# Block-sparse attention and a bilinear feed-forward: a planner's matmul times and margins taken anew

## The chip, the cores and the metric

The kernel runs on one core of a Trainium2 chip. Each engine of the core works through its own list of instructions in order: PE multiplies matrices, DVE and ACT work element by element and move results out of PE's accumulators, POOL gathers blocks of keys, SP and ACT issue DMA transfers. Engines wait for each other and for transfers on semaphores. The metric is the device time of one launch in microseconds (us). The median of three runs of the kernel before is 862.08 us (860.63 to 865.51).

## The reference

Four batches of eight heads attend over 768 positions with 64 numbers per head. Positions fall into 24 blocks of 32, and a block of queries sees few blocks of keys; what comes out is laid side by side into 3072 tokens of 512 numbers, and a feed-forward follows.

```
B, H, S, D = q.shape                       # 4, 8, 768, 64
scores = q @ k.transpose / sqrt(D)
mask = (|blk_i - blk_j| <= 1) or blk_i in (0, 23) or blk_j in (0, 23)
for qb in range(24):
    for kb in sampled_blocks[qb]:          # three random blocks
        mask[qb, kb] = True
attn = softmax(where(mask, scores, -1e9))
x = (attn @ v).reshape(3072, 512)
out = ((x @ w_a) * (x @ w_b)) @ w_out      # w_a, w_b: 512 x 1536, w_out: 1536 x 512
```

## The kernel before

Every matrix is held as a high and a low fp16 part, and each product is three matmuls (high by high, low by high, high by low). The work falls into two sorts.

**Attention** goes by units, one for each block of 32 queries of a batch with all eight heads: 96 units. Unit n of batch b has the name b*24+i; those with i = 0 and i = 23 are dense (all 24 key blocks), the others have eight gathered blocks. For a unit POOL gathers key columns (`KG`, L629 to L634), SP loads gathered value rows (`VG`, L656 to L669), PE makes scores (L1031 the mask, L930 the products: the task S), DVE takes a minimum (`low`), ACT the exponentials (`sm`, L1056), ACT and DVE split the weights into parts (`hl`, L948 to L955), the DMA or PE turns them (`pt`, L1081 or L1109), and PE multiplies them with the values (L974: the task A). Two helpers write the attention into `xT` (L1241 on ACT, L1244 on DVE).

**The feed-forward** goes by 12 chunks of 256 tokens (eight units), three of a batch, and by 12 slices of the inner dimension. Task P of a chunk and slice makes both first products in `ab` (L1273, 24 matmuls); ACT and DVE multiply them into `a` (L1290, L1293) and split the result into `gh` and `gl` (L1302, L1305); task O multiplies these with w_out (L1333 to L1335, 6 matmuls). P of a chunk needs all of the chunk's units. "P3_0" is chunk 3, slice 0; "A31" the values of unit 31. PE fills waits in one chunk's units with tasks of earlier chunks.

At the start the weights are loaded, put into 32-bit words from two halves (L775 to L782 on DVE), scaled, and split into parts (L806 to L823), slice by slice; keys and values of the first batch the same way; and tables of the sampled blocks are made (`make_tables`, L405: loads L421 to L428 on ACT's queue, then L433 to L463 on DVE). `offs`, which the gather of keys needs, comes from the first table, the mask `mrows` from the second. Weights of later slices are loaded and converted among the first units.

The order on each engine is not written by hand. When the kernel is built, a class `Plan` (L133) simulates all flows with given times: `pe(ns, fn)` asks for the matmul engine for so many ns, `dve`, `act`, `pool`, `sp` and `load_way` for the others. It picks what can start first, with a rank as the tie-break, and writes instructions in that order. On the chip the order is fixed, and real durations and real semaphores decide. The numbers in the plan never reach the chip. The constants `LATE_*` are margins: an event is said to be later than the simulated time by that much, so what needs it is put further back. `GATE_*` and `LEAD_*` say how many units ahead loads begin. The plan also models eight lanes of DMA transfers (`LANES`) and the two levels of PE's clock (`array`, L182).

```
at = max(ready, self.free.get(way.eng, 0.0))
if way.moved:
    at = max(at, self.dma - DMA_AHEAD, self.generator)
    if len(self.landed) >= LANES:
        at = max(at, self.landed[-LANES])
```

The transfers of the chip go by eight semaphores in turn (DMAHW0 to DMAHW7), so a transfer is issued only when the one that had the same semaphore eight issues earlier has landed, and an issue that has to wait holds up what is queued behind it on its engine.

Of the kernel before, what the change touches and what calls it, by code (L numbers as in the profile page):

```python
# [53 lines left out]

LATE_PT, LATE_VG, LATE_AV, LATE_G = 2500, 2500, 1500, 700
LATE_S = 1000
LATE_HL, LATE_KS, LATE_Q = 2500, 2500, 2000
DMA_AHEAD = 1750
X_HIGH, X_UNITS = 600, 16

# [180 lines left out]
def load_way(moved, fn):  # L241

    return [Way("LOAD", 475, fn, moved)]
# [7 lines left out]
def kernel(  # L251
# [238 lines left out]
    def keys(b, g):  # L490
        yield from gate(first_of[b] - GATE_KV)
        raw, freed = yield from raw_tile(b, g, 0)
        yield load_way(1000, lambda: nc.scalar.dma_start(raw, k[b, g]))
        if g + 1 < NG:
            plan.start(keys(b, g + 1), first_of[b] - LEAD_K)
        elif b > 0:
            plan.start(values(b, 0), first_of[b] - LEAD_V)
        t = raw.rearrange("p (t d) -> p t d", d=D)
        done = yield from take("ks", KS_BUFS)
        ks = work.tile([P, 2 * NT, P], F16, tag="ks", name=f"ks{b}_{g}", bufs=KS_BUFS)  # L500
        at = at_k + b * NG + g
        s = scale[:, at : at + 1]
        yield act(1020, lambda: nc.scalar.activation(
            ks[:, :, :D], t, AF.Abs, accum_out=bound[:, at : at + 1]
        ))
        end = yield from set_scale(slice(at, at + 1), FLOOR_QK)
        k_scale[b].fire(end)
        yield act(930, lambda: nc.scalar.activation(ks[:, :, :D], t, AF.Copy, scale=s))
        end = yield dve(1070, lambda: nc.vector.scalar_tensor_tensor(
            ks[:, :, D:], t, s, ks[:, :, :D], ALU.mult, ALU.subtract  # L510
        ))
        freed.fire(end)
        if b == 0:
            ends = Event(2)
            for h in range(2):
                plan.start(turn_keys(g, h, ks, ends, done), first_of[b] - LEAD_K, end)
            return
        if b == 1:
            yield w_freed
        if b >= 2:  # L520
            yield k_free[b - 2]
        end = yield sp(1700, 2200, lambda: nc.sync.dma_start_transpose(
            keysT[b % 2][:, 2 * g : 2 * g + 2, :].rearrange("p h (t s) -> p (h t) s", s=P),
            ks.rearrange("p t d -> p (t d)"),
        ))
        done.fire(end + LATE_KS)
        k_ready[b].fire(end + LATE_KS)
# [31 lines left out]
    def values(b, g):  # L559

        yield from gate(first_of[b] - GATE_KV)
        raw, freed = yield from raw_tile(b, g, 1)
        yield load_way(1000, lambda: nc.scalar.dma_start(raw, v[b, g]))
        if g + 1 < NG:
            plan.start(values(b, g + 1), first_of[b] - LEAD_V)
        elif b + 1 < B:
            plan.start(keys(b + 1, 0), first_of[b + 1] - LEAD_K)
# [21 lines left out]
            vd[b][:, g * 4 * D : (g + 1) * 4 * D].rearrange("(t p) x -> p t x", p=P),  # L589
            vs.rearrange("p t a x -> p t (a x)"),  # L590
        ))
        done.fire(end)
        v_stored[b].fire(end)

    def values_scale(b):
        yield v_bound[b]
# [136 lines left out]
    def turn_queries(cc, a):  # L733

        end = yield sp(650, 700, lambda: nc.sync.dma_start(
            QT[cc][D:, 1 - a], QT[cc][:D, a]
        ))
        q_ready[cc].fire(end)


    def raw_weights(n, count):
# [218 lines left out]
    def values_into(b, i, quads, first, last):  # L960
# [22 lines left out]
                for g in (2 * hq, 2 * hq + 1):  # L983
                    pair_sums(g, terms)

        t = yield pe(sum(len(terms) for _, terms in quads) * 180 + 80, sums)
        if last and quads[-1][0] == HQ - 1:
            av_done[b, i].fire(t)
            if i % 2:
# [24 lines left out]
    def attend(b, i):  # L1014
# [24 lines left out]
            for hq in range(HQ):  # L1039
                scores(ps[:, hq], cc, i, hq, lambda h: kg[:, h], False)  # L1040

        t = yield pe(850, all_scores)
        kg_free[kn].fire(t)
        next_unit(b, i, t - HOP)
        mx = low[:, at, :, 0]
# [85 lines left out]
    def attend_quad(b, i, hq, ends):  # L1131
# [14 lines left out]
            )  # L1146

        for x in range(2):
            t = yield pe(450, lambda x=x: half_scores(x))
        if hq == 0:  # L1150
            quad_sent[b, i].fire(t - HOP)
        else:
# [103 lines left out]
    def first_products():  # L1256
        plan.start(second_products(), R_P2)
        for cc, f in in_order:
# [18 lines left out]
                                skip_group_check=True,  # L1277
                            )

            t = yield pe(2680, products)  # L1280
            if f == NF - 1:
                ffn_done[cc].fire(t)
            plan.start(inner(cc, f, ab, read), R_NOW, t)
# [28 lines left out]
    def second_products():  # L1312
        banks, o_read = [None] * NJ, [None] * NJ
        sums = [{} for _ in range(NC)]
        for cc, f in in_order:
# [18 lines left out]
                    mm(po, gh[:, js], wol[:, f, :], start=False, stop=False)  # L1334
                    mm(po, gl[:, js], wos[:, f, :], start=False, stop=(f == hi - 1))  # L1335

            t = yield pe(1290, products)
            if f == hi - 1:
                for j in range(NJ):
                    plan.start(  # L1340
# [123 lines left out]
```

## Time and profile before

| | before |
|---|---|
| median of 3 runs | 862.08 us (860.63 to 865.51) |
| the profiled execution's own time | 856.35 us |
| its span, first to last instruction | 854.6 us |
| mean granted clock of PE | 0.966 of full speed |
| PE busy | 763.1 us (89%) |
| DVE busy | 587.0 us (69%) |
| ACT busy | 501.3 us (59%) |

All durations that follow are from the one profiled execution; its own time is 1.75 us above its span and 0.7% under the median. The span has three stages. In the first, up to some 190 us, weights and keys are converted while the first units run; in the second PE has attention and feed-forward tasks side by side; in the third, from some 750 us, only the feed-forward's last tasks are left.

### The profile page before, as it was taken

The numbers are of one execution on the slowest core, as the hardware profiler recorded it, in microseconds if no ns is written. First come the engines' busy times: TensorE is split into PE (matmuls) and PEld (weight loads), VectorE is DVE, ScalarE is ACT, GpSimd is POOL, SyncE is SP. The second block draws the span as 40 slices with busy tenths as digits, with TensorE's granted clock in tenths as the row PEclk, the third lists the DMA queues.
The fourth block names the chain that finished last, engine by engine and source line by source line (L and its number), as shares of the span: only waits on it lengthen the run. The fifth ranks groups of instructions, "written<-read, shape, count | busy, mean of one in ns | idle before, by whom it ended". The sixth has DMA issues, their size and how long they took to land.

```text
span 854.6 us, 24181 instructions
## 1 busy us (share of the span) xinstructions
PE 763.1 (89%) x9192; PEld 568.3 (66%) x9192; DVE 587.0 (69%) x1589; ACT 501.3 (59%) x1158; POOL 179.5 (21%) x428
## 2 busy tenths in 40 slices
PE   2256478799999979999999999999999999999998
PEld 1134366577767757767777867777777677777775
DVE  4999989998687568775677786755767876332222
ACT  6688779776675467684475765843845663232222
POOL 0642332300043133120034240200422310000000
PEclk9985589999999999999999999999999999999999
DMA  8767795577957589987676989667677767500000
GB/s 270 227 192 238 237 237 183 156 145 180 203 150 173 123 189 236 187 191 174 151 184 150 177 208 226 149 180 165 158 164 152 146 147 150 129 25 2 26 1 25
DMA packets 187758, 136.89 MB, mean 160 GB/s; under 512 B 130681, under 2 KB 155258, under 8 KB 187642
## 3 DMA queue, kind: packets, MB, share of 16 engines
q1 hardware_dynamic: 175712, 97.56, 51.7%
q10 hardware_dynamic: 11930, 37.79, 14.5%
q8 instruction: 72, 1.18, 0.6%
q14 instruction: 44, 0.36, 0.1%
HBM read 86.28 MB, written 12.58 MB: 116 GB/s over the span
## 4 chain that ended last, share of the span: by engine, by line
PE 62%; DVE 16%; DMA 9%; ACT 6%; issue 3%; SPq 2%; POOL 1%; ACTq 0%; POOLq 0%; DVEq 0%
PE ab L1273 33%; PE av L974 7%; PE o L1333 6%; PE o L1335 6%; PE o L1334 5%; PE s L930 4%; DMA VG<-vd 3%; DVE hl L955 2%; ACT sm L1056 2%; DMA keysT<-ks 2%; DVE xT L1244 2%; DVE low L1046 1%; DVE QT L711 1%; ACT QT L709 1%; PE s L1031 1%
## 5 line engine op out<-in xcount | busy, mean ns | idle before, releaser
L1273 PE MATMUL ab<-xT,wab 128*128 128x256 f16 x3456 | 403.8, 274 | 2.4 <-DVE a L1293 1.8
L1273 PEld LDWEIGHTS <-wab 128*128 128x128 f16 x3456 | 336.2, 98 | 67.8 <-issue 10.2
L1293 DVE SCALAR_TENSOR_TENSOR a<-a,to_g,ab 128x256 f32<-128x256 f32 x144 | 68.7, 478 | 116.5 <-ACT a L1290 115.0
L1290 ACT ACTIVATE a<-ab,w 128x256 f32<-128x256 f32 x144 | 67.3, 468 | 128.0 <-PE ab L1273 126.5
L1056 ACT ACTIVATE sm<-s,low,cq 128x256 f32<-128x256 f32 x176 | 97.8, 558 | 49.1 <-DVE low L1049 25.4
L629 POOL COPY KG<-keysT 128x384 int32<-128x384 int32 x88 | 57.0, 647 | 308.0 <-PE s L930 279.7
L974 PEld LDWEIGHTS <-VG 128*128 128x128 f16 x2688 | 99.2, 101 | 29.5 <-issue 20.2
L974 PE MATMUL av<-pt,VG 128*128 128x64 f16 x2688 | 105.4, 197 | 15.0 <-ACT pt L1115 6.9
L1333 PE MATMUL o<-woh,gh 128*128 128x512 f16 x288 | 109.7, 381 | 2.4 <-ACT gh L1302 2.4
L1335 PE MATMUL o<-wos,gl 128*128 128x512 f16 x288 | 109.2, 379 | 2.8 <-DVE gl L1305 2.8
L1334 PE MATMUL o<-wol,gh 128*128 128x512 f16 x288 | 109.2, 379 | 0.0
L955 DVE SCALAR_TENSOR_TENSOR hl<-sm,den,hl 128x256 f16<-128x256 f32 (+1 forms) x208 | 104.6, 510 | 3.3 <-ACT hl L948 1.5
L634 POOL COPY KG<-keysT 128x128 int32 x264 | 92.0, 385 | 45.2 <-issue 23.3
L1302 ACT ACTIVATE gh<-a 128x256 f16<-128x256 f32 x144 | 59.4, 413 | 57.6 <-DVE a L1293 55.0
L1305 DVE SCALAR_TENSOR_TENSOR gl<-gh,a 128x256 f16<-128x256 f16 x144 | 63.0, 438 | 29.7 <-ACT gh L1302 28.4
L1244 DVE SCALAR_TENSOR_TENSOR xT<-av,xT 64x256 f16<-64x256 f32 x96 | 40.4, 421 | 40.9 <-ACT xT L1241 40.1
L930 PE MATMUL s<-KG,QT 128*32 128x256 f16 x1408 | 59.6, 293 | 9.3 <-POOL KG L634 7.5
L1046 DVE TENSOR_REDUCE low<-s 128x2 f32<-128x512 f32 x88 | 60.0, 683 | 8.3 <-PE s L930 7.6
L1241 ACT ACTIVATE xT<-av 64x256 f16<-64x256 f32 x96 | 36.1, 376 | 42.5 <-PE av L974 41.3
L930 PEld LDWEIGHTS <-QT 128*32 128x32 f16 x1664 | 43.8, 102 | 18.2 <-issue 7.7
L1335 PEld LDWEIGHTS <-gl 128*128 128x128 f16 x288 | 28.1, 98 | 39.7 <-DVE gl L1305 6.9
L948 ACT ACTIVATE hl<-sm,den 128x256 f16<-128x256 f32 (+1 forms) x86 | 43.9, 514 | 9.9 <-DMA pt<-hl 2.5
(116 smaller groups left out, 771.7 us busy)
## 6 DMA issues: line engine op xcount, KB each, us to landing
VG<-vd SPq DMA_DIRECT2D x284, 64.0 KB, 2.3
VG<-vd SPq DMA_DIRECT2D x88, 192.0 KB, 3.1
VG<-vd SPq DMA_DIRECT2D x32, 384.0 KB, 3.7
q<-in_q_dram ACTq DMA_DIRECT2D x24, 256.0 KB, 5.1
QT<-QT SPq DMA_DIRECT2D x24, 256.0 KB, 3.3
vd<-vs SPq DMA_DIRECT2D x16, 384.0 KB, 3.1
out_dram<-ou SPq DMA_DIRECT2D x24, 256.0 KB, 2.3
stage<-in_k_dram ACTq DMA_DIRECT2D x12, 384.0 KB, 4.4
```

The lines of the kernel that those rows point to most:

```text
L634: nc.gpsimd.tensor_copy(to[:, :, (5 + r) * w : (6 + r) * w], of[:, :, bass.ds(at, w)])
L930: mm(to[h * BLK : (h + 1) * BLK], q_block(cc, i, 4 * hq + h, a), rhs(4 * hq + h), start=(first and a == 0), stop=(a == 1), skip_group_chec ...
L955: t = yield dve(221 + n * 1.03, lambda: nc.vector.scalar_tensor_tensor(lo, sm, over, hi, ALU.mult, ALU.subtract))
L974: mm(av[:, g, i % 2, :], w, pt[:, y, cols], start=(i % 2 == 0 and g == 0 and first and n + m == 0), stop=(last and n == len(terms) - 1 and ...
L1046: yield dve(685, lambda: nc.vector.tensor_reduce(mx, ps, axis=mybir.AxisListType.X, op=ALU.max, negate=True))
L1056: t = yield act(750, lambda hq=hq: nc.scalar.activation(sm[:, hq], ps[:, hq], AF.Exp, bias=low[:, at, hq, 0:1], scale=cq[:, cc, hq : hq + ...
L1273: mm(ab[:, i, :], wab[:, f, i, part, kt, :], xc[:, kt, a, :], start=(i == 0 and kt == 0 and part + a == 0), stop=(kt == KT - 1 and a == 1) ...
L1290: yield act(470, lambda: nc.scalar.activation(a_sb, ab[:, 0, :], AF.Copy, scale=w3[:, f : f + 1]))
L1293: t = yield dve(420, lambda: nc.vector.scalar_tensor_tensor(a_sb, a_sb, to_g[:, n : n + 1], ab[:, 1, :], ALU.mult, ALU.mult))
L1333: mm(po, gh[:, js], woh[:, f, :], start=(f == lo), stop=False)
L1334: mm(po, gh[:, js], wol[:, f, :], start=False, stop=False)
L1335: mm(po, gl[:, js], wos[:, f, :], start=False, stop=(f == hi - 1))
```

## The change

Times that the plan takes for PE's tasks are set anew, and margins are added or made longer. No instruction of the chip's is written differently; what changes is when the plan believes that things are ready, and with it the order of the instructions and which engine takes a step that can go to either.

```diff
-LATE_HL, LATE_KS, LATE_Q = 2500, 2500, 2000
+LATE_HL, LATE_KS, LATE_Q = 2500, 4000, 2000
+LATE_KV, LATE_VD, LATE_QT = 1500, 2000, 1000
...
         yield load_way(1000, lambda: nc.scalar.dma_start(raw, k[b, g]))
+        yield LATE_KV
...
         yield load_way(1000, lambda: nc.scalar.dma_start(raw, v[b, g]))
+        yield LATE_KV
...
-        done.fire(end)
-        v_stored[b].fire(end)
+        done.fire(end + LATE_VD)
+        v_stored[b].fire(end + LATE_VD)
...
-        q_ready[cc].fire(end)
+        q_ready[cc].fire(end + LATE_QT)
...
-        t = yield pe(sum(len(terms) for _, terms in quads) * 180 + 80, sums)
+        t = yield pe(sum(len(terms) for _, terms in quads) * 165 + 60, sums)
...
-        t = yield pe(850, all_scores)
+        t = yield pe(690, all_scores)
...
-            t = yield pe(450, lambda x=x: half_scores(x))
+            t = yield pe(385, lambda x=x: half_scores(x))
...
-            t = yield pe(2680, products)
+            t = yield pe(2650, products)
...
-            t = yield pe(1290, products)
+            t = yield pe(1310, products)
```

Three places show what becomes of the order. Lines of the kernel after are one to three higher than before. The numbers at the end of names tell buffers apart and differ between the two.

The first place is ACT's list in the first microseconds. Before, behind the loads of values (`wab_73<-in_v_dram`):

```order
L563 DMA wab_73<-in_v_dram 128x768
L508 ACTIVATE ks0_1_123<-wab_73,scale_94 128x12x64
L563 DMA wab_73<-in_v_dram 128x768
L421 DMA mrow_118<-in_sampled_blocks_dram 1x144
L425 DMA mbox_117<-in_sampled_blocks_dram 24x6
L428 DMA mbox_117<-c_blocks 24x29
L755 DMA stage_77<-in_moe_w_a_dram 128x1024
L508 ACTIVATE ks0_2_125<-wab_73,scale_94 128x12x64
```

After, behind the copies of the transposed keys (`keysT0`), and ahead of the second slice's weights:

```order
L574 ACTIVATE va0_2_247,bound_v_92<-wab_73 128x768
L758 DMA stage_77<-in_moe_w_a_dram 128x1024
L809 ACTIVATE wab_73,bound_91<-wab_73 128x2x512
L422 DMA mrow_118<-in_sampled_blocks_dram 1x144
L426 DMA mbox_117<-in_sampled_blocks_dram 24x6
L429 DMA mbox_117<-c_blocks 24x29
L758 DMA stage_77<-in_moe_w_b_dram 128x1024
L809 ACTIVATE woh_74,bound_91<-w2_196 128x512
```

The three loads of the sampled blocks and constants (`mrow`, `mbox`) stood between conversions of keys (`ks0`), and now stand behind the Square of the first slice of weights (L809, before L806). On DVE the table work that follows them stood ahead of the first weights, and now stands behind them.

The second place is ACT's list at the units 8 to 12 of the first batch, with the semaphores that a row waits for. `stage_77` and `keysT1_79` are where weights land, `q2` the queries of chunk 2, `sm11` the exponentials of unit 11. Before:

```order
L693 DMA q2_1406<-in_q_dram 64x1024 [waits DMAHW4_49]
L693 DMA q2_1406<-in_q_dram 64x1024 [waits DMAHW7_49]
L811 ACTIVATE woh_74<-w17_1088,scale_94 128x512
L948 ACTIVATE hl9_1409<-sm9_1344,den_98 128x256 [waits DMAHW6_49,Activation_49]
L823 ACTIVATE wos_76<-woh_74 128x512 [waits Activation_49]
L948 ACTIVATE hl9_1409<-sm9_1344,den_98 128x256
L948 ACTIVATE hl10_1418<-sm10_1376,den_98 128x256 [waits DMAHW1_49,DVE_49]
L755 DMA stage_77<-in_moe_w_b_dram 128x1024 [waits DMAHW3_49]
L1056 ACTIVATE sm11_1495,den_98<-s11_1372,low_97,cq_96 128x256 [waits DVE_49,PE_49]
L1056 ACTIVATE sm11_1495,den_98<-s11_1372,low_97,cq_96 128x256
```

After:

```order
L696 DMA q2_1404<-in_q_dram 64x1024 [waits DMAHW3_49]
L696 DMA q2_1404<-in_q_dram 64x1024 [waits DMAHW4_49]
L951 ACTIVATE hl9_1409<-sm9_1335,den_98 128x256 [waits DVE_49,Activation_49]
L758 DMA stage_77<-in_moe_w_b_dram 128x1024 [waits DMAHW6_49,DMAHW0_49]
L814 ACTIVATE wab_73<-wab_73,scale_94 128x2x512 [waits DVE_49]
L758 DMA stage_77<-in_moe_w_out_dram 128x1024 [waits DMAHW7_49,DVE_49]
L951 ACTIVATE hl9_1409<-sm9_1335,den_98 128x256 [waits Activation_49]
L951 ACTIVATE hl8_11_1408<-sm8_11_1262,den_98 128x384
L814 ACTIVATE woh_74<-w17_1152,scale_94 128x512
L809 ACTIVATE woh_74,bound_91<-w20_1224 128x512
L1059 ACTIVATE sm11_1500,den_98<-s11_1371,low_97,cq_96 128x256 [waits DVE_49,PE_49]
L951 ACTIVATE hl10_1432<-sm10_1378,den_98 128x256 [waits DMAHW1_49]
```

The load of w_b stood directly ahead of `sm11` and now stands seven rows ahead of it, with conversions and the load of w_out between them, and it waits for other lanes.

The third place is ACT's list around the end of chunk 2's slices (`a2_9` to `a2_11`, `gh2_9` to `gh2_11`) and the units 35 to 38 (`sm35` ...), shortly ahead of chunk 3's first product. Before:

```order
L1302 ACTIVATE gh2_11_5294<-a2_11_5237 128x256
L1056 ACTIVATE sm35_5315,den_98<-s35_5101,low_97,cq_96 128x256 x2
L1360 ACTIVATE ou2_0_5339<-o2_0_0_4165,to_out_104 128x512
L704 ACTIVATE QT5_5242,bound_91<-q5_5178 64x2048
L1056 ACTIVATE sm36_5420,den_98<-s36_5191,low_97,cq_96 128x256 x2
L1241 ACTIVATE xT0_88<-av1_6_5290 64x4x64 x2
L1056 ACTIVATE sm37_5456,den_98<-s37_5331,low_97,cq_96 128x256
L878 ACTIVATE junk_105,bound_91<-xT0_88 128x1024
L493 DMA stage_77<-in_k_dram 128x768
L709 ACTIVATE QT5_5242<-q5_5178,scale_94 64x2048
L1056 ACTIVATE sm37_5456,den_98<-s37_5331,low_97,cq_96 128x256
```

After:

```order
L1293 ACTIVATE a2_9_5235<-ab2_9_5026,w3_99 128x256
L1059 ACTIVATE sm36_5282,den_98<-s36_5094,low_97,cq_96 128x256
L1305 ACTIVATE gh2_9_5289<-a2_9_5235 128x256
L1059 ACTIVATE sm36_5282,den_98<-s36_5094,low_97,cq_96 128x256
L1293 ACTIVATE a2_10_5280<-ab2_10_5236,w3_99 128x256
L712 ACTIVATE QT5_5107<-q5_5095,scale_94 64x2048
L1305 ACTIVATE gh2_10_5350<-a2_10_5280 128x256
L951 ACTIVATE hl34_5284<-sm34_5043,den_98 128x256
L1293 ACTIVATE a2_11_5375<-ab2_11_5290,w3_99 128x256
L494 DMA stage_77<-in_k_dram 128x768
L1244 ACTIVATE xT0_88<-av1_6_5182 64x4x64 x2
L951 ACTIVATE hl35_5293<-sm35_5208,den_98 128x256
```

Before, the last slice's `gh2_11` stood ahead of `sm35`; now `gh2_9` to `gh2_11` stand among and behind `sm36`. On PE the order before was A30, S37, A31, S38, P3_0; after it is A30, S37, P2_11, S38, A31, two O tasks of chunk 2, A32, P3_0, and then the last O task of chunk 2.

## Rows read from the trace of the kernel before

**Rows 1.** Busy us by stretch: PE, PEld, DVE, ACT, POOL, PEclk, DMA share, GB/s.

```profile
100.00:150.00 50.00, 39.44 (x516) 30.25 (x516) 45.87 (x119) 41.32 (x90) 15.35 (x31) 0.86 0.74 209
...
200.00:750.00 550.00, 537.58 (x6759) 400.63 (x6755) 384.45 (x1079) 321.51 (x780) 119.64 (x309) 1.00 0.77 170
```

**Rows 2.** Waits of PE, 200 to 750 us: line, releaser, us, times, longest.

```profile
PE av L974 <- DMA VG<-vd: 3.3, 6, 1.0
PE o L1333 <- ACT gh L1302: 2.2, 2, 1.7
PE s L930 <- DMA QT<-QT: 1.9, 3, 1.3
PE ab L1273 <- DVE a L1293: 1.8, 2, 1.2
PE s L1031 <- ACT sm L1056: 1.0, 2, 0.8
PE o L1335 <- DVE gl L1305: 0.9, 2, 0.6
PE av L974 <- DMA pt<-hl: 0.8, 2, 0.4
PE ab L1273 <- DVE xT L1244: 0.6, 1, 0.6
```

**Rows 3.** Timeline of ACT, the start: issues of table loads; first weight Square.

```profile
10.71 0.54 ACTq L421 DMA_DIRECT2D mrow<-in_sampled_blocks_dram  x1
...
28.65 1.06 ACT L806 ACTIVATE wab<-wab 128x1024 f16<-128x1024 f32 x1 [0.56 <-DVE wab L782]
```

**Rows 4.** Timeline of DVE, the start.

```profile
17.57 0.17 DVE L433 TENSOR_SCALAR mrow<-mrow 1x72 f32<-1x72 int32 x1
...
20.91 0.28 DVE L463 CAST mrows<-mbox 24x256 bf16<-24x256 f32 x1
...
34.39 0.67 DVE L1046 TENSOR_REDUCE low<-s 128x2 f32<-128x512 f32 x1
...
36.70 2.96 DVE L584 SCALAR_TENSOR_TENSOR vs<-wab,scale,vs 128x768 f16<-128x768 f32 x3
...
44.77 0.51 DVE L955 SCALAR_TENSOR_TENSOR hl<-sm,den,hl 128x256 f16<-128x256 f32 x1
```

**Rows 5.** Timeline of PE, the start.

```profile
31.21 1.04 PE L930 MATMUL s<-KG,QT 128*32 128x256 f16 x16 [4.57 <-POOL KG L634]
```

**Rows 6.** Groups of DVE by line and shape, 0 to 165 us: busy, mean ns.

```profile
L951 DVE TENSOR_SCALAR hl<-sm,den 128x256 f16<-128x256 f32 x7 | 2.4, 348 | 0.1
...
L550 DVE COPY keysT<-kt 128x768 f16<-128x768 f16 x4 | 2.2, 546 | 0.0
...
L1116 DVE COPY pt<-pt_t 128x1024 f16<-128x1024 f16 x2 | 1.4, 685 | 0.0
L951 DVE TENSOR_SCALAR hl<-sm,den 128x384 f16<-128x384 f32 x3 | 1.3, 431 | 0.0
```

**Rows 7.** Timelines at 114 us: ACT, and last DVE.

```profile
114.33 0.35 ACTq L755 DMA_DIRECT2D stage<-in_moe_w_b_dram  x1
114.79 0.56 ACT L1056 ACTIVATE sm<-s,low,cq 128x256 f32<-128x256 f32 x1 [5.39 <-DMA VG<-vd]
...
116.02 0.17 DVE L1061 TENSOR_SCALAR den<-den 128x2 f32<-128x2 f32 x1 [3.56 <-ACT sm L1056]
```

**Rows 8.** Timeline of PE, 308 to 317 us.

```profile
308.45 0.39 PE L1333 MATMUL o<-woh,gh 128*128 128x512 f16 x1 [1.70 <-ACT gh L1302]
...
312.88 0.77 PE L974 MATMUL av<-pt,VG 128*128 128x64 f16 x21 [0.95 <-DMA VG<-vd]
...
316.29 2.97 PE L1273 MATMUL ab<-xT,wab 128*128 128x256 f16 x16 [0.60 <-DVE xT L1244]
```

**Rows 9.** Busy us in ten-us stretches, columns as in rows 1.

```profile
300.00:310.00 10.00, 8.00 (x122) 5.41 (x119) 5.62 (x15) 4.45 (x13) 2.99 (x10) 1.00 1.06 191
310.00:320.00 10.00, 7.64 (x117) 5.74 (x116) 7.71 (x25) 9.13 (x19) 3.90 (x10) 0.83 0.72 195
```

## The prediction, made before the result was known

> **What bounds the kernel now.** I read the busy times by stretch first, because the stages have different limits. From 100 to 150 us DVE is busy 45.87 of 50 us and PE 39.44, at a granted clock of 0.86: here DVE's list of conversions sets the pace, and PE waits for it. From 200 to 750 us PE is busy 537.58 of 550 us, at full clock [rows 1]. In that middle stage a change of order can win only what PE waits, 12.4 us. The waits of PE there say for what: 3.3 us for gathered values, 2.2 for `gh`, 1.9 for queries turned by DMA, 1.8 for `a`, 1.0 for exponentials, 0.9 for `gl`, 0.8 for turned weights, 0.6 for `xT` [rows 2], which add up to 12.5 us. What is left after 750 us is matmuls without a partner; no number of the change reaches it. So there are three places to look at: the start, where the order on ACT and DVE counts; the long stall that ACT shows in its timeline near 114 us; and PE's waits in the middle, of which a third lie in eight microseconds, as the timeline of PE shows.
>
> **The start.** Before, the load of the sampled blocks is issued at 10.71 us [rows 3] and the tables' first conversion starts at 17.57 us, so it has taken at most 6.9 us until it could be used; the last table row starts at 20.91 and ends at 21.19 [rows 4], so the block is some 3.6 us long. After, ACT issues that load behind the first Square of the weights. This Square starts at 28.65 us before [rows 3]; without the tables ahead of its input it can start up to 3.6 us sooner, at some 25 us, and the issue follows at some 26. With 6.2 to 6.9 us until use, three short conversions (0.5 us) and a gather of 4 us (PE waited 4.57 us for the one ahead of the first scores [rows 5]), S0 starts at some 37.4 us in place of 31.21, 6.2 us later. What hides part of that is that DVE has work, and it now does it first: 2.96 us of conversions of values stand before S0's reduction that stood behind it, and two conversions of weights (1.5 us, between 34.39 and 36.70) as well. The distance from S0's reduction (34.39) to the second half of `hl0` (44.77) [rows 4] shrinks by these 4.5 us, and the lag there is 6.2 - 4.5 = 1.7. In the DVE-bound stage that is what counts. I take +1.7, with bounds of 0 (the load lands fast and DVE is never idle) and +6.2 (all of the lag stays).
>
> **Conversions that go to the other engine.** Steps that ACT or DVE can do are put down anew. Up to chunk 1's first product DVE loses one copy of keys (0.546 us), four conversions of `hl` of 0.348, two copies of `pt` of 0.685 and two conversions of dense `hl` of 0.431, in all 4.17; it gains one copy of `pt` and five of `hl`, 2.42 [rows 6]. DVE is lighter by 1.75 us, ACT heavier by some 2 to 3 us. ACT is busy 41.32 of 50 us where DVE is busy 45.87 [rows 1], so the ACT work finds room. I take -1.75; bounds -1.75 and 0.
>
> **The stall at 114 us.** ACT stands idle 5.39 us ahead of `sm11`, put down to a load of gathered values; the row before it is the issue of w_b's load at 114.33 [rows 7], which has to wait for the transfer eight issues earlier. `sm11` is queued behind the issue, DVE's L1061 needs its sums and waits 3.56 us for them [rows 7]. In a stage that DVE bounds, that is the price. After, the load of w_b stands seven rows ahead of `sm11` and waits for an earlier transfer, since the lanes fall otherwise. What can be late next is the load of w_a behind `sm11`, which waits for a query load, ahead of chunk 2's `QT`. I take 0.8 us of the 3.56 as left: -2.8; bounds -3.6 and 0.
>
> These three make -2.85 for the start of the middle stage.
>
> **The chunk boundary at 308 to 317 us.** PE waits 1.70 us for `gh`, 0.95 for the values of unit 31, 0.80 for exponentials and 0.60 for `xT` ahead of chunk 3's first product, 4.05 us in eight [rows 2, 8]. The new order puts P2_11 between S37 and A31, and A31, two O tasks and A32 ahead of P3_0: between the write of `xT` by unit 31 and P3_0 there is now PE work of two O tasks and a unit's values, where there was one S. That covers 0.60, and 0.95 is covered by P2_11. `gh2_11` no longer stands alone in front: O tasks of chunk 2 are left over as fill. I take 3.3 of the 4.05 as gone; bounds 0 and -4.05. Behind this cluster the granted clock falls: 0.83 in the stretch 310 to 320 and 1.00 ahead [rows 9]. That is 3.4 us at the lower level, 1.7 lost. It comes with a PE that was busy 8.00 and then 7.64 of ten us. If the cluster goes, I expect this to go: -1.7; bounds -1.7 and +1.7 (another such fall elsewhere).
>
> **The other waits in the middle.** Of 3.3 + 1.9 + 0.8 us for values, queries and turned weights [rows 2], 0.95 is in the cluster; 5.05 are left. The new margins (values stored and turned queries later in the plan) and shorter times of A and S let the plan issue more of the attention ahead, so that most loads of values have more PE work behind them. I take half: -2.5; bounds 0 and -5.05. Against that stands that every order has waits of its own that its plan does not see, and a fresh order has fresh ones: the old one has 12.5 us in 550. Take from it the 3.3 and 2.5 that I count as gone, and 6.7 remain; that the new order brings half as many again, +3.5, is my choice; the bounds are 0 and +12.5 (as many as before, all new).
>
> A rule of the Trainium skill bears on this. Rows first: in 300 to 310 us the DMA engines are busy 1.06 of their time by the records, while PE waits for values at 312.88 [rows 8, 9]. "DMA: Bandwidth & Descriptors", section "Issuing engines are not separate DMA queues", says that transfers started by any of the engines run on the same 16 DMA engines and interleave. By it the lateness would be a matter of bytes in that stretch and not of the order of issue, and the -0.95 and the -2.5 would not come; that case is a rival below.
>
> **The sum.** 1.7 - 1.75 - 2.8 - 3.3 - 1.7 - 2.5 + 3.5 = -6.85 us. The profiled execution took 856.35 us, which becomes 849.5; the ratio is 0.992. The profiled execution was 0.7% faster than the median of the runs shown, so I put the ratio on the median: 862.08 x 0.992 = 855.2 us. The best end: no lag at the start, -1.75, -3.6, all 12.5 of the waits, -1.7, in all -19.55, by the same ratio 842.4 us.
>
> **The rivals.**
> *No change.* The gain at 114 us and the one at the boundary come, but waits come back elsewhere, because the DMA engines are the limit around 300 to 340 us (1.06 busy, above) and because a later S0 eats the start: 1.7 - 1.75 - 2.8 - 1.5 (half of the boundary and nothing of the clock) + 4 of new waits = -0.35, so 861.7 us. For it: the DMA share in the middle is 0.77 over 550 us [rows 1], and the bytes are the same. Against it: 0.77 is no limit over the whole, only in stretches.
> *Slower.* The late tables. Its place is S0: when the load of the sampled blocks lands as late as I worked out, the whole lag of 6.2 us goes through DVE, because each unit needs S, `sm` and `hl` one after the other. Nothing else gained: 862.08 x (856.35 + 6.2)/856.35 = 868.3 us. It decides if DVE stands idle for more than 4 us between 25 and 45 us. For it: where DVE sets the pace [rows 1], each microsecond in which it has nothing to do is lost. Against it: the 4.5 us of work moved ahead.
> *A large gain.* All waits of the middle go: 842 to 845 us. Against it: no order so far is free of waits.
>
> **Chances.** The forecast 0.50, no change 0.25, the late tables 0.20, the large gain 0.05. A measurement of this kernel can tell about 0.5% (4.3 us) from no change, so faster means below 857.8 and slower above 866.4. The forecast with its own range of 849 to 859 lies in "faster" with 0.45 and in "same" with 0.05; the late tables give 0.18 to "slower" and 0.02 to "same". Faster 0.45 + 0.05 = 0.50, same 0.05 + 0.25 + 0.02 = 0.32, slower 0.18. The range goes from the middle of the large gain, 844, to the late tables' 868.
>
> **What would show it.** In the profile after: S0 starts at about 37 us, with DVE idle for about 2 us ahead of it; ACT has no idle row above 2 us between 105 and 120 us; the first product of chunk 3 starts some 6 to 9 us sooner than 316.29 [rows 8], and the stretch that holds it has a granted clock of 1.00 and PE busy above 9 of ten; PE's waits from 200 to 750 us add up to 8 to 10 us. It would be wrong if `hl0`'s second half came more than 4 us later than 44.77, if the w_b load, or the w_a load behind `sm11`, stood on ACT's queue for 3 us again, or if the waits for values in the middle grew above 6 us.

## The result, and the profile after

| | before | after |
|---|---|---|
| median, 4 runs of each in one comparison | 863.63 us (860.63 to 865.51) | 850.43 us (850.02 to 857.9) |
| ratio of the runs | 1 | 0.988 (0.9834 to 0.9926) |
| the profiled execution's own time | 856.35 us | 850.74 us |
| its span | 854.6 us | 849.0 us |
| PE busy in the span | 763.1 us (89%) | 759.4 us (89%) |

The kernel is 1.2% faster; 855.2 us had been forecast. The spans of the two profiles differ by only 5.6 us where the medians differ by 13.2, since the profiled execution of before was shorter than any of its four runs here. Both kernels were therefore profiled a second time (experiments 9 and 12). A ratio leaves out runs over 1.5% longer than the fastest of the same kernel in that comparison (none here, three of six in experiment 11, whose median of all six is 861.62 us).

The busy times by stretch of the kernel after, with the columns of [rows 1]; the first two answer to the two shown of before:

```profile
100.00:150.00 50.00, 35.07 (x454) 27.03 (x444) 42.13 (x107) 37.09 (x81) 18.55 (x33) 0.72 0.86 186
200.00:750.00 550.00, 546.33 (x6895) 409.29 (x6894) 386.47 (x1086) 331.75 (x802) 121.65 (x309) 1.00 0.77 172
100.00:130.00 30.00, 15.07 (x189) 11.18 (x179) 23.88 (x61) 17.82 (x38) 12.19 (x20) 0.56 1.04 199
300.00:350.00 50.00, 48.80 (x651) 36.34 (x649) 37.45 (x114) 33.32 (x82) 15.79 (x41) 1.00 0.93 205
350.00:750.00 400.00, 398.20 (x5080) 299.61 (x5079) 273.30 (x768) 231.50 (x568) 81.98 (x208) 1.00 0.74 166
```

From 100 to 150 us PE is busy 35.07 us in place of 39.44, and the granted clock is 0.72 in place of 0.86: the start became worse, against the forecast. From 200 to 750 us PE is busy 546.33 in place of 537.58: the middle gained 8.75. The last three rows are for comparison with the same stretches before:

```profile
100.00:130.00 30.00, 21.25 (x258) 15.95 (x259) 26.09 (x70) 22.44 (x49) 11.88 (x24) 0.77 0.88 233
300.00:350.00 50.00, 44.86 (x653) 32.87 (x650) 39.08 (x116) 34.13 (x85) 18.12 (x47) 0.97 0.98 213
350.00:750.00 400.00, 393.27 (x5015) 294.88 (x5014) 269.98 (x761) 228.62 (x562) 78.16 (x204) 1.00 0.75 166
```

PE lost 6.2 us of busy time from 100 to 130 us and gained 3.9 and 4.9 us in the two stretches behind 300. Where [rows 8, 9] have 15.64 us of 20 and the waits ahead of chunk 3, from 300 to 320 us, PE is now busy 20.00 of 20 at full clock, and no row of its timeline there has a wait:

```profile
300.00:310.00 10.00, 10.00 (x148) 7.87 (x146) 6.57 (x21) 6.43 (x16) 2.45 (x9) 1.00 0.78 175
310.00:320.00 10.00, 10.00 (x129) 7.52 (x128) 9.22 (x22) 7.66 (x16) 4.29 (x9) 1.00 1.07 212
```

What is left of PE's waits from 200 to 750 us answers to [rows 2]:

```profile
PE av L977 <- DMA pt<-hl: 1.9, 3, 0.7
PE av L977 <- DMA VG<-vd: 1.7, 2, 0.9
```

These are 3.6 us where there were 12.5. The waits for `gh`, `gl`, `a`, `xT`, exponentials and queries are gone.

The timelines of the start, with the rows that answer to [rows 3 to 5]:

```profile
26.66 0.48 ACTq L422 DMA_DIRECT2D mrow<-in_sampled_blocks_dram  x1
...
31.28 0.18 DVE L434 TENSOR_SCALAR mrow<-mrow 1x72 f32<-1x72 int32 x1
...
38.05 0.28 DVE L464 CAST mrows<-mbox 24x256 bf16<-24x256 f32 x1
...
46.62 0.47 DVE L958 SCALAR_TENSOR_TENSOR hl<-sm,den,hl 128x256 f16<-128x256 f32 x1
...
38.38 0.35 PE L1034 MATMUL s<-mrows,ident 128*32 128x192 bf16 x4 [14.44 <-DVE mrows L464]
38.49 1.09 PE L933 MATMUL s<-KG,QT 128*32 128x256 f16 x16
```

The table load went from 10.71 to 26.66 us, the tables are done at 38.3 in place of 21.2, and the first products of scores start at 38.49 (forecast 37.4, before 31.21). `hl0` is at 46.62 in place of 44.77: of the 7.3 us 1.9 are left, and 1.7 had been forecast.

What answers to [rows 7] are the timelines of ACT, SP and PE from 104 to 117 us:

```profile
104.43 0.40 ACTq L758 DMA_DIRECT2D stage<-in_moe_w_a_dram  x1
...
106.88 0.50 ACTq L758 DMA_DIRECT2D stage<-in_moe_w_b_dram  x1
...
110.00 0.34 ACTq L758 DMA_DIRECT2D stage<-in_moe_w_out_dram  x1
...
116.66 0.51 ACT L951 ACTIVATE hl<-sm,den 128x256 f16<-128x256 f32 x1 [3.49 <-DMA pt<-hl]
...
105.00 1.22 SPq L1199 DMA_TRANSPOSE pt<-hl  x1
...
116.68 1.12 PE L977 MATMUL av<-pt,VG 128*128 128x64 f16 x18 [7.74 <-DMA pt<-hl]
```

The load of w_b is issued at 106.88 and holds nothing up. But now three loads of 512 KB, at 104.43, 106.88 and 110.00, stand close by the turn of dense unit 8's weights. (Units are named in the order in which they are handled, and batch 0 begins with its chunk 1; so unit 8 is the dense block i = 0, and b*24+i holds from batch 1 on.) The turn is issued at 105.00, and PE waits 7.74 us for it until 116.68; the chain of waits has it as one piece, from the issue to the landing:

```profile
105.00 11.63 DMA pt<-hl
```

In the kernel before the turns at this place landed 2.7 to 4.4 us after their issue. ACT stands idle 3.49 us on the same transfer. The stall changed its form and its length.

### The profile page after: what moved, and what is told of

Same layout as the page of the kernel before. It is cut to its first block, busy times and chain, and to the rows that moved or that the text cites. A ratio compares the mean times of both kernels' runs of the same rounds, so it can differ in the third digit from the quotient of the medians.

```text
span 849.0 us, 24214 instructions
## 1 busy us (share of the span) xinstructions
PE 759.4 (89%) x9192; PEld 568.1 (67%) x9192; DVE 583.7 (69%) x1580; ACT 505.9 (60%) x1167; POOL 187.0 (22%) x428
## 4 chain that ended last, share of the span: by engine, by line
PE 65%; DVE 14%; DMA 9%; ACT 6%; issue 3%; SPq 2%; POOL 1%; POOLq 0%; ACTq 0%; DVEq 0%
PE ab L1276 34%; PE av L977 7%; PE o L1336 6%; PE o L1338 6%; PE o L1337 6%; PE s L933 4%; DMA pt<-hl 4%; DMA VG<-vd 2%; DVE hl L958 2%; DMA QT<-QT 1%; PE s L1034 1%; DVE QT L714 1%; DVE low L1049 1%; DVE xT L1247 1%; DVE wab L819 1%
## 5 line engine op out<-in xcount | busy, mean ns | idle before, releaser
L632 POOL COPY KG<-keysT 128x384 int32<-128x384 int32 x88 | 59.0, 670 | 308.7 <-PE s L933 284.2
L1059 ACT ACTIVATE sm<-s,low,cq 128x256 f32<-128x256 f32 x176 | 97.9, 559 | 42.7 <-DVE low L1052 24.8
L637 POOL COPY KG<-keysT 128x128 int32 x264 | 98.1, 409 | 40.2 <-POOL KG L632 26.6
L951 ACT ACTIVATE hl<-sm,den 128x256 f16<-128x256 f32 (+1 forms) x94 | 47.8, 519 | 17.8 <-DMA pt<-hl 6.8
L1034 PE MATMUL s<-mrows,ident 128*32 128x192 bf16 (+1 forms) x352 | 25.9, 283 | 29.5 <-DVE mrows L464 14.4
```

What stands on the lines that cost most here:

```text
L637: nc.gpsimd.tensor_copy(to[:, :, (5 + r) * w : (6 + r) * w], of[:, :, bass.ds(at, w)])
L1059: t = yield act(750, lambda hq=hq: nc.scalar.activation(sm[:, hq], ps[:, hq], AF.Exp, bias=low[:, at, hq, 0:1], scale=cq[:, cc, hq : hq + ...
```

## The experiments

The expectations speak of PE's loss: the time up to a point less the matmul work that PE had started by then, each task at its duration at full clock. It is matched from the records to the list of tasks, and the records slip against it in places (in experiment 1 above all). A plain count of the matmul records up to a point, each at its spacing at full clock, gives the differences between kernels that are used below to within some 0.5 us. Where the two could differ I read PE's busy time and granted clock by stretch instead. The verdicts are ratios to the kernel before, run beside it on the same chip.

**1. The five PE times alone**

```diff
# in the kernel before
-        t = yield pe(850, all_scores)
+        t = yield pe(690, all_scores)
... (and the four others of the change; all margins as before)
```

> The kernel before with the five PE times of the change alone, all margins as before. The change's trace lost 9.1 us of PE's time (time less the work at full clock) between 200 and 750 us, the kernel before 21.3; up to 200 us 106.3 against 99.6. Theory (the middle is won by PE times that fit the measured ones, the start is lost by the margins): the loss in the middle is 9 to 12 us, that up to 200 us 97 to 101, the run 846 to 851 us, ratio to before 0.980 to 0.988. Rival (the middle is won by the margins): the middle loses 18 to 22 us, ratio 0.997 to 1.003.

Measured 0.9984 (0.9951 to 1.0018): no change. The stretches 300 to 350 and 350 to 750 us:

```profile
300.00:350.00 50.00, 39.80 (x576) 29.97 (x576) 37.37 (x114) 30.22 (x75) 16.13 (x41) 0.91 0.95 197
350.00:750.00 400.00, 398.30 (x4995) 297.12 (x4988) 274.02 (x780) 226.46 (x553) 86.67 (x212) 0.99 0.73 163
```

From 350 us PE is busy 398.30 of 400, as in the kernel after and 5 us more than before. From 300 to 350 it is busy 39.80, 5 us less than before, at a lower clock (0.91). So the PE times do win the long stretch, and alone they lose the same at the boundary. The theory held for half; the ratio is the rival's.

**2. The margins alone**

```diff
# in the kernel after
-        t = yield pe(690, all_scores)
+        t = yield pe(850, all_scores)
... (and the four others back)
```

> The kernel after with the five PE times of before; margins as after. Theory: the margins bring the late tables, so S0 starts at 37 to 39 us and the loss up to 200 us is 103 to 108 us, while the middle loses 15 to 21 us as before: ratio to before 1.000 to 1.010. Rival (the margins win the middle): the middle loses 8 to 12 us, ratio 0.985 to 0.995.

Measured 1.0167 (1.0115 to 1.0219), slower than the theory had it. The stretches 300 to 350 and 350 to 750 us:

```profile
300.00:350.00 50.00, 44.30 (x614) 31.74 (x615) 35.24 (x105) 32.18 (x79) 14.38 (x37) 0.90 0.84 178
350.00:750.00 400.00, 383.71 (x4931) 285.21 (x4923) 271.29 (x785) 227.46 (x561) 84.08 (x216) 1.00 0.80 168
```

383.71 us from 350 to 750 us is the least of all profiles. The rival is refuted: the margins alone win nothing in the middle.

**3. No margin behind the first batch's loads**

```diff
-        yield LATE_KV
+        yield LATE_KV * (b > 0)
```

> The kernel after, with the margin behind the loads of keys and values left out for the first batch alone (it stays for batches 1 to 3). The table loads then stand where they stood before, and S0 starts at 30 to 32 us in place of 38.4. Theory (the late tables cost the 1.8 us that the prediction took, the stall at 108 to 117 us is a second thing): the loss at 100 us is 1 to 2 us under the 77.9 of the change, and what comes at 105 to 130 us depends on where the loads stand; ratio to before 0.978 to 0.988. Rival (the late tables carry all of the 6.7 us): the loss at 200 us falls from 106.3 to 99 to 100, ratio 0.978 to 0.982.

Measured 1.013 (1.0083 to 1.0177). The tables are early (the mask's matmuls run at 25.6 us, the first products at 30.49), and that is worth 1.7 us at 100 us, as forecast. At 200 us the kernel is 9.5 us ahead, more than the rival had; but what comes between 100 and 200 us stands in another order too, so that part is not shown to be the tables'. All of it and more is lost behind 300 us:

```profile
300.00:350.00 50.00, 33.46 (x492) 25.59 (x491) 31.22 (x99) 27.01 (x66) 12.94 (x34) 0.76 0.83 177
```

33.46 busy of 50 at a clock of 0.76. A better start made a slower kernel; neither theory had that.

**4. Three loads of weights held**

```diff
             freed.append((yield from take("w", W_BUFS)))
+            if m in (24, 26):
+                yield 8000
```

> The kernel after, with the three loads of weights (512 KB each) that ACT issues at 104.4, 106.9 and 110.0 us held back by 8 us in the plan; they then stand behind sm11 to sm12 on ACT, the rest of the list up to there stands as it was. Theory (the turned weights of dense unit 8, 11.6 us from issue to landing, stand in the DMA engines behind these loads): PE's wait of 7.74 us for pt goes to 3 us or less, the transposes land in 3 to 6 us, the loss at 130 us falls by 3 to 6 us against the change; ratio to before 0.978 to 0.986. Rival (the transposes are late for their own reason: the queue of SP, or their lane): the wait stays at 6 to 8 us.

Measured 1.0045 (1.0009 to 1.0082). The stretches, and PE's timeline at the wait that was 7.74 us:

```profile
100.00:130.00 30.00, 23.25 (x297) 18.60 (x297) 28.09 (x78) 23.85 (x56) 15.10 (x25) 0.75 0.77 194
300.00:350.00 50.00, 35.31 (x529) 26.64 (x527) 32.84 (x102) 30.04 (x73) 11.40 (x34) 0.83 0.80 175
```

```profile
111.08 1.12 PE L979 MATMUL av<-pt,VG 128*128 128x64 f16 x18 [4.08 <-DMA pt<-hl]
```

The wait is 4.08 us (3 or less was expected), and one of 4.26 stands ahead of it. The turns land 4.3 to 6.7 us after their issue, where the kernel after has 2.8 to 12.9; the DMA engines are busy 0.77 of their time from 100 to 130 us in place of 1.04, and PE is busy 23.25 us there in place of 15.07. So the three loads cost PE that time. That they do it by standing ahead of the turns in the DMA engines is borne out in part (see experiment 8). Again the gain is lost at 300 us: 35.31, clock 0.83.

**What 1, 3 and 4 have in common.** All lose 9 to 15 us of PE's work from 300 to 350 us against the kernel after, whatever the start was like. The traces have one difference between the kernel after and experiments 1 to 4. The staging buffer for a chunk's queries exists once (`rq`), and the last slice's weights (w33) use the same one. In the kernel before, the queries of chunk 3 take it first. The timelines of ACT and DVE before:

```profile
187.94 0.48 ACTq L693 DMA_DIRECT2D q<-in_q_dram  x1
...
207.96 1.21 DVE L782 SCALAR_TENSOR_TENSOR w<-keysT,w 128x1024 int32<-128x1024 int32 x1
...
209.21 0.81 ACTq L493 DMA_DIRECT2D stage<-in_k_dram  x2
```

The queries are loaded at 187.94, w33 is converted up to 209.17 (the first stage goes on to there, and not to some 190 us), and in the same microsecond the loads of batch 1's keys are issued, which have to wait until all weights are converted (`w_freed`). After:

```profile
195.05 1.22 DVE L785 SCALAR_TENSOR_TENSOR w<-keysT,w 128x1024 int32<-128x1024 int32 x1
...
196.31 1.04 ACTq L494 DMA_DIRECT2D stage<-in_k_dram  x2
...
203.12 0.48 ACTq L696 DMA_DIRECT2D q<-in_q_dram  x1
```

w33 comes first, is done at 196.27, and the key loads are issued at 196.31, 12.9 us sooner. The queries come behind them. In experiments 1 to 4 the queries had it first again.

**5. The kernel after, with the queries first**

```diff
# in queries(cc), behind take("rq", 1)
+        if cc == 3:
+            q3_in.fire(0)
# in weights(n), ahead of its take("rq", 1)
+            if n == 33:
+                yield q3_in
```

> The kernel after, and one rule more: chunk 3's queries take the single large staging buffer ahead of the last slice's weights (w33), as in the kernel before and in the first four experiments; DVE's list is the same up to that place. New theory (what the change wins is this swap: with w33 first the last weights are converted at 196.3 us in place of 209.2, the keys of batch 1 are loaded in the same microsecond, its units stand further ahead, and PE still has chunk 2's tasks when it has to wait for chunk 3): the key loads start at 207 to 213 us, PE loses 8 to 17 us between 300 and 350 us in place of 2.1, the run is 858 to 870 us, ratio to before 0.998 to 1.008. Rival (the gain belongs to the PE times and margins of the change, spread over the middle): ratio 0.984 to 0.990 as the change has it.

Measured 1.0166 (1.0115 to 1.0217): 875.81 us, slower than expected. ACT's timeline and the stretch:

```profile
214.23 0.81 ACTq L495 DMA_DIRECT2D stage<-in_k_dram  x2
```

```profile
300.00:350.00 50.00, 37.85 (x502) 28.46 (x500) 30.86 (x91) 24.92 (x62) 11.58 (x32) 0.80 0.69 158
```

The key loads come 17.9 us later than in the kernel after. DVE's list is the kernel after's up to w33. One swap of two flows at one buffer turns 0.988 into 1.017.

**6. The kernel before, with w33 first**

```diff
# in queries(cc), ahead of take("rq", 1)
+        if cc == 3:
+            yield w33_in
# in weights(n), behind its take("rq", 1)
+            if n == 33:
+                w33_in.fire(0)
```

> The kernel before, with w33 ahead of chunk 3's queries in the single buffer and nothing else changed; DVE's list is the same up to that place. New theory: the key loads of batch 1 start at 196 to 201 us, the loss from 300 to 350 us falls from 8.2 to 1 to 4 us, and the run is 4 to 9 us shorter, ratio 0.989 to 0.996. Rival (the swap alone is worth nothing without the new times): ratio 0.997 to 1.005.

Measured 1.0093 (1.0059 to 1.0128): a miss, and slower than before. The key loads come at 194.25 us, a little sooner than expected, but PE is busy 45.04 us from 300 to 350 (before 44.86) and 387.05 from 350 to 750. The waits ahead of chunk 3 are gone, though; what PE waits for from 300 to 350 us is one new thing, the turned queries ahead of chunk 5's first unit:

```profile
321.32 1.05 PE L935 MATMUL s<-KG,QT 128*32 128x256 f16 x16 [4.96 <-DMA QT<-QT]
```

So this order costs 0.9% with the old PE times, and part of that is a stall of its own. What the swap is worth with the old times and without this stall was not tried.

**7. The PE times alone, with w33 first** (the diffs of 1 and 6)

> The kernel before with the five PE times alone (0.998 of before by itself) and w33 ahead of chunk 3's queries. New theory: tables early, PE's loss up to 130 us 87 to 88 us, the loss from 300 to 350 us 1 to 4 us in place of 17, the run 838 to 848 us, ratio 0.974 to 0.984, and so ahead of the change. Rival: 0.990 to 1.000.

Measured 1.004 (1.0001 to 1.0078): a miss. The boundary has 44.97 us of PE work in place of 39.80. But at 242 us there is a new stall, as the timelines of ACT and PE show:

```profile
215.26 1.13 ACTq L696 DMA_DIRECT2D q<-in_q_dram  x2
...
227.97 1.90 ACT L707 ACTIVATE QT<-q 64x2048 f16<-64x2048 f32 x1
...
242.18 0.83 PE L935 MATMUL s<-keysT,QT 128*32 128x384 f16 x16 [3.59 <-DMA QT<-QT]
```

The queries of chunk 3 are now issued behind three loads of batch 1's values, and used 12.7 us later; batch 1's first scores wait for them. In the stretch 220 to 230 us the DMA engines are busy 1.26 of their time:

```profile
220.00:230.00 10.00, 6.87 (x71) 5.55 (x70) 1.83 (x3) 5.30 (x10) 0.00 (x0) 0.99 1.26 193
```

**8. Held loads and w33 first** (the diffs of 4 and 6, on the kernel after)

> The kernel after with the three loads of weights held (1.0045 of before by itself) and w33 ahead of chunk 3's queries. New theory: the loss at 130 us is 87 to 89 us as with the held loads alone, the loss from 300 to 350 us 2 to 5 us in place of 18.7, ratio 0.976 to 0.986. Rival (the late start is what lets the attention of batch 1 get ahead, so a better start is lost again at 300 to 350 us): the loss there is 7 us or more, ratio 0.985 to 0.993.

Measured 0.9836 (0.9797 to 0.9874), 848.16 us. As the theory had it:

```profile
100.00:130.00 30.00, 21.66 (x284) 17.16 (x284) 26.93 (x74) 21.93 (x52) 12.18 (x24) 0.74 0.76 168
300.00:350.00 50.00, 48.05 (x637) 35.62 (x635) 37.62 (x114) 34.27 (x81) 16.30 (x42) 0.97 0.84 208
350.00:750.00 400.00, 396.78 (x5016) 297.55 (x5014) 270.97 (x761) 233.35 (x570) 78.87 (x203) 1.00 0.74 162
```

The start is as good as before (21.66 from 100 to 130 us), and the middle as good as after. The rival, that a better start is lost again, is refuted for this order. The stall itself is shorter and not gone. With the three loads held the turns land 3.1 to 10.3 us after their issue, and PE still waits for one:

```profile
112.86 1.12 PE L984 MATMUL av<-pt,VG 128*128 128x64 f16 x18 [6.64 <-DMA pt<-hl]
```

The loads are thus a part of the lateness of the turns. What the rest is, no run shows.

**9. The kernel after again**, unchanged.

> The kernel after, unchanged, beside the others of this call. All theories: ratio to before 0.985 to 0.992. The loss of PE up to 200 us, from 300 to 350 us and from 350 to 750 us is read once more: 106, 2 and 6 us in its first profile.

Measured 0.988 (0.982 to 0.9939), median 855.04 us beside 863.66 of before. The three stretches again:

```profile
100.00:130.00 30.00, 16.31 (x237) 13.23 (x237) 24.58 (x64) 20.39 (x42) 13.96 (x24) 0.67 1.01 239
300.00:350.00 50.00, 46.91 (x596) 34.44 (x594) 35.74 (x107) 32.47 (x79) 14.00 (x34) 0.97 0.90 198
350.00:750.00 400.00, 394.59 (x5034) 296.18 (x5032) 272.79 (x769) 230.04 (x564) 80.42 (x208) 1.00 0.76 166
```

PE is busy 1.9 and 3.6 us less in the last two than in the first profile of the same kernel; its waits from 200 to 750 us add up to 8.4 us in place of 3.6.

**10. As 7, with the queries ahead of the values**

```diff
# in values(b, g)
+        if b == 1 and g == 0:
+            yield q3_sent
```

> The seventh experiment (PE times alone, w33 first; 1.004 of before), and the first load of batch 1's values waits in the plan until chunk 3's queries have been issued. In the seventh the queries were issued at 215.3 us behind three loads of values and first used at 228.0, and PE lost 9.3 us from 225 to 250 us. Theory (the transfers were bunched; queries ahead of the values land in 4 to 8 us): PE loses 0 to 3 us from 225 to 250 us, the run is 5 to 10 us shorter than the seventh, ratio 0.990 to 0.998. Rival (the queries are late because w33 took their buffer, wherever the values stand): that loss stays at 7 us or more, ratio 1.000 to 1.008.

Measured 0.9878 (0.9825 to 0.9931), 13 us under experiment 7, more than expected. ACT's timeline:

```profile
210.50 1.25 ACTq L699 DMA_DIRECT2D q<-in_q_dram  x2
...
216.60 1.89 ACT L712 ACTIVATE QT<-q 64x2048 f16<-64x2048 f32 x1
```

The queries are used 6.1 us after their issue. The loss from 225 to 250 us is 5.7 us and not 0 to 3, so the landing is halved and the stall is not gone. PE is busy 48.67 and 397.63 us behind 300. This kernel has the old margins: with the right two orders the new margins aren't needed.

**11. As 8, without the margin behind the loads of keys and values**

```diff
-LATE_KV, LATE_VD, LATE_QT = 1500, 2000, 1000
+LATE_KV, LATE_VD, LATE_QT = 0, 2000, 1000
```

> The eighth experiment (the kernel after, three loads of weights held, w33 first; 0.9836 of before) without the margin behind the loads of keys and values, so that the tables are loaded early again. Theory (the late tables cost 1 to 2 us of PE at the start, and no more, and the middle keeps its gain as long as w33 is first): S0 at 24 to 27 us, the loss at 100 us 76 to 77 us in place of 77.4, ratio 0.978 to 0.986. Rival (any fresh order has its own waits, and these weigh more than the tables): the loss from 200 to 750 us is 18 us or more in place of 12.7, ratio 0.990 to 1.005.

Measured 0.9856 (0.9777 to 0.9934), an interval twice as wide as that of experiment 8; the two can't be told apart. The mask's matmuls run at 24.8 us, the first products at 29.74, and the loss at 100 us is 75.8 against 77.4: the late tables cost 1.6 us. But PE is busy 44.98 and 392.47 us behind 300: the rival holds as well, the fresh order has waits of its own.

**12. The kernel before again**, unchanged, for a second profile.

> The kernel before, unchanged, for a second profile of it: its first was taken of an execution of 856.35 us, faster than most of its timed ones (852.7 to 868.0, median 861.6). Theory (the profile of before was a lucky one, and what it lacks against the others lies at the same places, the start and 300 to 350 us): an execution of 858 to 866 us, PE's loss up to 200 us 100 to 104 us, from 300 to 350 us 8 to 11 us, from 350 to 750 us 12 to 15 us. Rival (the executions differ by the granted clock in the start alone): the loss up to 200 us is 104 us or more, the rest within 1 us of the first profile.

Measured 1.0 (0.9952 to 1.0048). The profiled execution has a span of 865.6 us, 11 more than the first:

```profile
100.00:130.00 30.00, 22.02 (x257) 16.57 (x258) 25.66 (x69) 21.93 (x49) 10.99 (x21) 0.70 0.89 226
300.00:350.00 50.00, 43.60 (x638) 32.16 (x637) 37.33 (x114) 34.00 (x86) 16.57 (x42) 1.00 0.95 196
350.00:750.00 400.00, 388.48 (x4982) 290.53 (x4980) 274.77 (x775) 229.68 (x567) 80.50 (x211) 1.00 0.79 169
```

It lost 3 us more by 200 us, and PE is busy 2.1 us less from 200 to 300 and 4.8 less from 350 to 750, spread over many waits. The theory holds for the start; its second place, 300 to 350 us, does not hold: the waits ahead of chunk 3 are the same cluster, and most of the rest was lost behind it. The rival doesn't hold either. The stretch with the cluster shows one thing more:

```profile
310.00:320.00 10.00, 6.39 (x128) 4.42 (x126) 7.01 (x19) 6.81 (x17) 2.81 (x8) 1.00 0.87 207
```

PE is busy less than in the 7.64 us of [rows 9], and the granted clock stays at 1.00 (there 0.83).

## Why the prediction was right, and where it wasn't

The PE busy times of all profiles, by the two things that the experiments separated (mean of the profiles, us):

| PE times | first in the buffer | profiles | 300 to 350 | 350 to 750 | sum |
|---|---|---|---|---|---|
| old | queries | before twice, 2 | 44.3 | 388.5 | 432.7 |
| old | w33 | 6 | 45.0 | 387.1 | 432.1 |
| new | queries | 1, 3, 4, 5 | 36.6 | 394.5 | 431.1 |
| new | w33 | after twice, 7, 8, 10, 11 | 47.1 | 395.5 | 442.5 |

At 300 to 350 us the granted clock was 0.76 to 0.91 in the third line, and 0.90 to 1.00 in the others. In these means the gain needs both. The new PE times order the long stretch better by 6 to 8 us, and with the queries first they lose as much at the boundary to chunk 3. With w33 first batch 1 starts its keys 13 us sooner and the boundary is fed. Single profiles scatter: from 300 to 350 us the third line has 33.5 to 39.8 and the fourth 45.0 to 48.8, but from 350 to 750 us the first line's best (393.3) lies above the third's worst (390.2). And the second line is one profile, with the stall shown under experiment 6; that the swap is worth nothing with the old times is not shown.

The change did not ask for the swap; it fell out of the whole set of numbers. That with the new PE times the order at the buffer decides is shown by experiment 5 from one side and by 4 against 8 from the other, and experiment 10 shows that the new PE times and the right orders are enough without the margins. That it works through batch 1's keys is read from the same four traces. With the queries first the key loads come 17.9 us later (5 against the kernel after) and 15.7 us later (4 against 8), the first scores of batch 1 14.3 and 15.4 us later, the first product of chunk 3 16.0 and 17.0 us later. The weights w33 themselves, which the swap moves too, were not missed: from 200 to 300 us PE is busy 98.4 to 99.9 of 100 us in all four. What in an order with the new PE times makes PE run out of chunk 2's tasks sooner was not tried by itself.

The steps, one by one:

- *The start* (+1.7): right in size, by another path. The lag of `hl0` is 1.9 us (2.2 in the second pair of profiles), and experiment 11 gives 1.6 for the tables by themselves. But the load was in use after at most 4.6 us and not 6.2 to 6.9, and the gather ahead of the first scores was done at some 36 us. What came last was the mask, 38.3 us, behind 2.86 us of conversions of values on DVE, which had no idle row ahead of it.
- *Conversions to the other engine* (-1.75): nothing here shows it by itself; it lies under what follows.
- *The stall at 114 us* (-2.8): wrong, and the largest error. The step that failed was the reading that an issue which no longer blocks ACT leaves nothing behind. The loads that were let go stand beside the turned weights, and PE's busy time from 100 to 130 us fell by 6.2 us (5.7 in the second pair of profiles, 22.02 to 16.31). Holding the three loads gives that back, in experiments 4 and 8. How they do it is shown in part. PE's waits for turned weights from 90 to 130 us add up to 0.7 and 0.8 us in the two profiles of before, 13.9 and 14.0 in those of after, and 8.3 and 9.4 in experiments 4 and 8. So the loads account for some 5 of 13 us; the cause of the rest stays open. Some 4 us of the stall's cost are left at the end, by experiment 8 against the change (0.9836 and 0.988, with intervals that overlap).
- *A rule that I had weighed*: "DMA: Bandwidth & Descriptors" of the Trainium skill, section "Issuing engines are not separate DMA queues", says that transfers of all issuers share the same 16 engines. The traces agree from 100 to 130 us, where the DMA share is 1.04 and falls to 0.77 with the three loads held, and in experiment 7 from 220 to 230 us, where it is 1.26. At the place that I weighed a high share alone made no wait: from 310 to 320 us it is 1.07 in the kernel after, and PE is busy 10.00 of 10.
- *The chunk boundary* (-3.3): right in size. From 300 to 350 us PE is busy 44.86 us before and 48.80 after, 43.60 and 46.91 in the second pair, and the waits ahead of chunk 3 are gone but for 0.53 us in one. The mark for it held in one pair only: I took 316.29 us for the start of chunk 3's first product, whose first two matmuls ran at 315.10, and it came at 317.04 after; in the second pair it came 6.2 us sooner (320.79 and 314.64). And the reason was only half seen: I read that batch 1 stood ahead, not which buffer put it there.
- *The clock* (-1.7): right in the first pair by luck. I tied the fall of the clock to the waits ahead of chunk 3. The second profile of before has these waits and no fall, as the row under experiment 12 shows; the second profile of after has a fall without them (0.83 from 320 to 330 us, behind a wait of 2.56 us for values).
- *The other waits in the middle* (-2.5 and +3.5, together +1.0): mis-sized. From 350 to 750 us PE gained 4.9 us of busy time in the first pair and 6.1 in the second (388.48 to 394.59). PE's waits from 200 to 750 us went from 12.5 to 3.6 and from 20.3 to 8.4, where 8 to 10 was the mark. The waits for values, of which I took half, went from 3.3 to 1.7 and from 4.8 to 5.3; what shrank in both pairs are those for `gh`, `a` and exponentials. PE times nearer to what the trace shows (a unit's scores take 0.63 us, 690 ns in the new plan and 850 in the old) are worth more than I took, and experiment 2 shows the price of the old ones.
- *The rivals*: the late tables carried 1.6 us and not 6.2. "No change" saw that waits would come back at crowded DMA engines, but put them at 300 to 340 us, and was wrong in the sum.

So the number was right by two errors of opposite sign, which is luck. By PE's loss, mean of two profiles each, the change cost 4.0 us up to 200 us (before 99.6 and 102.7, after 106.3 and 104.0; the two pairs give 6.7 and 1.3) where -2.85 had been forecast, and from 200 to 750 us it won 12.8 (before 21.3 and 29.5, after 9.1 and 16.1; 12.2 and 13.4) where the terms gave 4.0.

## What to carry to other kernels

Where a build-time planner sets the order, find the single buffers that two flows share and look who takes each first: such a choice can turn 1.2% won into 1.7% lost while every constant stays as it is. When a wait on a lane or an issue goes, count the bytes that are set free and ask which small, urgent transfer they will meet. A gain at the start can be lost at the next point at which all engines meet (here 300 us), so look there too, and one profile of each kernel is not enough for differences of 1%.

## What the runs showed of the hardware

- Two executions of the same kernel had spans of 854.6 and 865.6 us, and PE's waits from 200 to 750 us were 12.5 us in one and 20.3 in the other. 23 runs of the kernel before in one comparison lay between 852.7 and 868.0 us.
- A turn of weights by DMA (fp16, 128x768) landed 2.8 to 12.9 us after its issue within one execution of the kernel after, from 90 to 120 us, and 2.7 to 4.4 us in the kernel before.
- The mean granted clock of an execution says little here: the profiled run of after had 0.939 and took 850.74 us, another had 0.976 and took 857.9.
